# The joint between the two layers of the second MLP: earlier first inputs, later differences and stores, later weight loads, and inputs issued by SyncE

## The chip, the cores and the metric

The kernel runs on one core of a Trainium2 chip. The metric is the device time of one execution in microseconds (us); lower is better. Each kernel is timed in several runs, and one further execution is profiled.

## The reference, cut to what matters

Linear attention over 32 heads, then two MLPs, all in float32:

```python
def phi(x):
    proj = einsum('bhsd,df->bhsf', x, w_phi)
    proj = proj - max(abs(proj), axis=-1)
    return concat([exp(proj), exp(-proj)], axis=-1)
q_p, k_p = phi(q), phi(k)                       # batch 4, 8 heads, 576 tokens, head size 64
num = einsum('bhsf,bhfd->bhsd', q_p, einsum('bhsf,bhsd->bhfd', k_p, v))
x = num / (einsum('bhsf,bhf->bhs', q_p, k_p.sum(2))[..., None] + 1e-6)   # -> 2304 x 512

h = x @ moe_w_in;   x = maximum(0.01 * h, h) @ moe_w_out                 # 512 -> 2048 -> 512
h = x @ moe2_w_in                                                        # 512 -> 2048
sp = where(h > 20, h, log1p(exp(minimum(h, 20))))
out = (h * tanh(sp)) @ moe2_w_out                                        # 2048 -> 512
```

The function between the second MLP's layers, h * tanh(softplus(h)), is called Mish below.

## The kernel before

Every float32 operand of a matmul is cut into a high and a low part, and a product is three matmuls: high by high, high by low, low by high (`three`, lines 95 to 97 of the profile). ScalarE (ACT) rounds the high part (line 91 for inputs, line 262 for weights) and VectorE (DVE) subtracts it to get the low part (line 92 and line 266); this pair is called a split.

The MLPs use a two-by-two block scheme with seven products in place of eight, so sums and differences of blocks stand in for the blocks. The change is about the second MLP. Its first layer runs in 16 items, `cycle(n)`, one for each of eight pairs f of feature blocks and two groups sb of tokens; the last two are item 14 (f = 7, sb = 0) and item 15 (f = 7, sb = 1). The seven products of an item are spread over two calls of `cycle`: the item's last three, `tail4`, `tail5` and `tail3`, run inside the next item. For item 15 they run after the loop, in `first`, with the product `c_item(7)` for the 256 left-over tokens in two halves around `tail3(15)`.

When a block of the first layer is done, ACT applies Mish (line 1424). Three of the four blocks of an item, B11, B21 and B22, are stored to DRAM at once. B12 stays in the tile `g12` (`x1_1`). As soon as the fourth block has come, DVE makes four differences T1, T3, T2, T4 in place (line 1444), and each is stored as well. All these stores are line 1418 (`put`): SyncE (SP) issues the differences, ACT the blocks. In the order listings their targets are called gp, then the group sb, then a number for the block (0 B11, 1 T3, 2 T2, 3 B21, 4 T1, 5 T4, 6 B22), then f // 2. `tail5` also has a DVE addition (line 843) whose result must find a free tile, and such a tile is free when its difference has been stored.

The second layer (`emit_s`) then runs 56 steps, s = 0 to 55, and 8 more for the left-over tokens. A step is 12 matmuls on one input of 128 x 1024 values. The input of step s is read back from DRAM into one of five places (`RAW3`, line 1472, called raw), split in two (called g2), and multiplied with the halves of one block of output weights (called wo2). Step 0 is called input 0 below, and so on. Weights for the last six of the seven phases come as 24 loads of 256 KB (line 1365, called wr), issued by SP into a ring of seven tiles, so that the load of wr n waits for the split of wr n-7.

What sets the order is a counter: each call of `work` is one position, and `later(k, f)` runs f k positions on. The order in which the program emits instructions is the order in which each engine runs them, and each DMA issue stands in its engine's order too. A DMA that has to wait for its source, its target or the DMA issued eight before it (their completion marks are eight, used in turn) holds its engine. The lines that matter: `later(s + 2, lambda s=s: then.load(s))` asks for the first inputs one item before the end, `deep = 3` lets three of them go ahead, and `later(2, lambda: free.add("s0"))` lets the weight loads begin.

Of the kernel before, what the change touches and what calls it, by code (L numbers as in the profile page):

```python
# [20 lines left out]
def attention_two_mlps_kernel(  # L21
# [12 lines left out]
    nc = tc.nc  # L34
# [25 lines left out]
    NF = M // 2  # L60
# [238 lines left out]
    with tc.manual_schedule():  # L299
# [1046 lines left out]
        for f in range(NF):  # L1346
# [3 lines left out]

        PHASES = ((A11, B11, "X"), (S3, T3, "Z"), (S2, T2, "Y"), (A12, B21, "X"), (S1, T1, "Y"), (A22, T4, "W"), (S4, B22, "Y"))
        HOMES = ["s%d" % i for i in range(6, 2 * OPS)] + ["x2_0", "x2_1", "x3_0", "x3_1"] + ["v%d" % i for i in range(9, 14)] \
            + ["xc"] + ["v%d" % i for i in range(4)] + ["x0_0", "x0_1"]
        homes, ready = Lane(5), Lane(1)
        lanes += (homes, ready)
        ready.queue.append(Chain((Stage(0.0, lambda: free.add("v4"), gate="l2",
# [63 lines left out]
        def mish(key, h, g=None):  # L1420
            m, b = key
            if g is None:
                g = role(key)
            nc.scalar.activation(out=g, in_=h, func=AF.Mish)
            if b == B:
                l = gl2[m] = dr.tile([P, 3, NC], F32, name="gl%d" % m)
                later(1, lambda: nc.scalar.dma_start(out=l[:, 0:2].rearrange("p a n -> p (a n)"), in_=g))

                def diff():
                    nc.vector.tensor_tensor(out=g[:, 0:NC], in0=g[:, NC:], in1=g[:, 0:NC], op=ALU.subtract)  # L1430
                    later(1, lambda: nc.sync.dma_start(out=l[:, 2], in_=g[:, 0:NC]))
                later(5, diff)
                return
            f, sb = m // 2, b // 2
            x = mine.setdefault((f, sb), {})
            x[m % 2, b % 2] = g
            if (m % 2, b % 2) != (0, 1):
                o = {(0, 0): B11, (1, 0): B21, (1, 1): B22}[m % 2, b % 2]
                later(1, lambda: put(sb, o, f, g))
                return  # L1440
            b11, b12, b21, b22 = x[0, 0], x[0, 1], x[1, 0], x[1, 1]
            for n, (o, out_, in0, in1) in enumerate(((T1, b11, b12, b11), (T3, b12, b22, b12), (T2, b22, b22, b11), (T4, b21, b21, b22))):
                def sub(o=o, out_=out_, in0=in0, in1=in1):
                    nc.vector.tensor_tensor(out=out_, in0=in0, in1=in1, op=ALU.subtract)
                    later(1, lambda: put(sb, o, f, out_))
                later(n + 1 + (n > 1), sub)

        two_.out, two_.dest = mish, role

        steps3 = [(sb, n, fp) for sb in range(2) for n in range(OPS) for fp in range(NF // 2)] + [(2, 0, f) for f in range(NF)]  # L1450
        NS3 = len(steps3)
        RAW3 = [("cc", gp), ("st0", gp), ("st1", gp), ("x1_0", fix), ("x1_1", fix)]
        PARTS3 = (("s0", "s1"), ("s2", "s3"), ("s4", "s5"))

        class Halves:
# [5 lines left out]
            def load(self, upto):  # L1461
                while self.loaded <= min(upto, NS3 - 1) and self.loaded - self.split_at < self.deep:
# [4 lines left out]
                    t = self.raw[s] = place(tag, F32, 2, MAIN, pool=pool, name="raw2").rearrange("p a n -> p (a n)")  # L1467
                    if sb == 2:
                        t = self.raw[s] = t[:, 0:3 * NC]
                        nc.scalar.dma_start(out=t, in_=gl2[fp].rearrange("p a n -> p (a n)"))  # L1470
                    else:
                        nc.scalar.dma_start(out=t, in_=gs2[sb, PHASES[n][1], fp].rearrange("p a n -> p (a n)"))

            def splits(self, upto):
                while self.split_at <= min(upto, NS3 - 1):
# [115 lines left out]
        def first(n, loads_at, then, few):  # L1591
            for x in items[n + (n > 0):] if n else items:
                if x[0] == "w" or n == 1 and cur[0] is one:
                    cycle(n)
                    n += 1
                    if n == len(it) - 1:
                        for s in range(6):
                            later(s + 2, lambda s=s: then.load(s))
                        if not few:
                            for f in range(NF):  # L1600
                                need("o2", f)
                    loads_at(n)
                if x[0] == "c" and x[1] < NF - 1:
                    c_item(x[1])
# [51 lines left out]

        def gates2(n):
            if n == len(it) - 1:
                later(2, lambda: free.add("s0"))
            if n == len(it):  # L1660
                later(2, lambda: free.add("s1"))

# [67 lines left out]
```

## Time and profile before

| | us |
|---|---|
| median of 3 runs (917.79 to 919.83) | 918.72 |
| the profiled execution | 920.56 |
| its span, first to last instruction | 918.6 |
| TensorE busy in the span | 897.2 (98%) |
| VectorE busy | 625.7 (68%) |
| ScalarE busy | 503.8 (55%) |

The profiled execution is 1.84 us over the median, and 1.96 us of it lie outside the span. Times in rows count from the start of the span. In a timeline a row is: start, length, engine, line, operation, result<-operands, count, and in brackets the idle time ahead of it and what ended that. PE is TensorE, SPq and ACTq are DMA issues of SyncE and ScalarE; the length of a merged row of issues includes the waits between them.

### The profile page before, as it was taken

To read this page: it belongs to the slowest core of one execution; us is meant where nothing else is said; L and a number is where in the kernel's file an instruction comes from. 1 tells how busy PE (TensorE), PEld (TensorE's weight loads), DVE (VectorE), ACT (ScalarE), POOL (GpSimd) and SP (SyncE) were. 2 spreads that over 40 slices of the span, in tenths; PEclk is the share of its full clock that TensorE was granted. 3 is DMA by queue.
4 is the path that set the end of the run, shared out by engine and by line. 5 is a ranking of instruction groups with operands and counts; after the bars stand their busy time and mean duration, and the time that the engine had idled before them with its cause. 6 is when DMAs were issued, how large, how long until landed. Compare 5 with 4: busy or idle time off the path is not lost.

```text
span 918.6 us, 17001 instructions
## 1 busy us (share of the span) xinstructions
PE 897.2 (98%) x6549; PEld 768.5 (84%) x6549; DVE 625.7 (68%) x1056; ACT 503.8 (55%) x827; POOL 68.7 (7%) x36
## 2 busy tenths in 40 slices
PE   8999999999999999999999999999999779999998
PEld 7999999888888888888988888888888658888888
DVE  7899999388888725889882328766654467655552
ACT  5888889566665545454463335544444456454441
POOL 3443443000000000000000000000000000000000
PEclk9999999999999999999999999999999989999999
DMA  7444430258878778799842365889655798886772
GB/s 210 126 102 113 136 106 16 93 182 279 310 262 303 268 226 278 242 356 377 281 137 95 115 218 195 308 300 325 244 218 188 275 364 285 236 238 196 221 195 61
DMA packets 146624, 199.37 MB, mean 217 GB/s; under 512 B 50928, under 2 KB 83312, under 8 KB 146544
## 3 DMA queue, kind: packets, MB, share of 16 engines
q1 hardware_dynamic: 107776, 112.82, 38.6%
q10 hardware_dynamic: 38768, 85.48, 27.2%
q8 instruction: 51, 0.84, 0.4%
q14 instruction: 29, 0.24, 0.1%
HBM read 120.65 MB, written 77.59 MB: 216 GB/s over the span
## 4 chain that ended last, share of the span: by engine, by line
PE 85%; DMA 6%; DVE 4%; ACT 2%; issue 1%; POOL 0%; ACTq 0%; SPq 0%; DVEq 0%
PE a L95 13%; PE a L96 13%; PE a L97 13%; PE b L95 12%; PE b L96 12%; PE b L97 12%; PE outs L491 3%; PE kvp L468 3%; DMA gp<-g 2%; PE a L384 1%; DMA c<-scr 1%; DMA gd<-g 1%; PE xt L516 1%; PE kvp L471 1%; DMA wr<-qd 1%
## 5 line engine op out<-in xcount | busy, mean ns | idle before, releaser
L92 DVE TENSOR_TENSOR g<-raw,g 128x1024 fp32r<-128x1024 f32 (+1 forms) x64 | 76.0, 1189 | 76.5 <-ACT g L91 76.2
L91 ACT ACTIVATE g<-raw 128x1024 fp32r<-128x1024 f32 (+1 forms) x64 | 66.1, 1033 | 81.6 <-PE b L97 39.4
L92 DVE TENSOR_TENSOR gl<-raw,gh 128x512 fp32r<-128x512 f32 x72 | 49.7, 690 | 65.9 <-ACT gh L91 64.7
L91 ACT ACTIVATE gh<-raw 128x512 fp32r<-128x512 f32 x72 | 45.2, 629 | 69.9 <-PE b L97 23.0
L451 POOL PARTITION_ALL_REDUCE qm<-qd x32 | 68.5, 2187 | 88.0 <-ACT qd L446 74.4
L96 PE MATMUL b<-gl,wo 128*128 128x512 f32 (+1 forms) x192 | 68.0, 354 | 0.1
L95 PE MATMUL b<-gh,wo 128*128 128x512 f32 (+1 forms) x192 | 67.9, 354 | 0.0
L97 PE MATMUL b<-gh,wo 128*128 128x512 f32 (+1 forms) x192 | 67.9, 354 | 0.0
L95 PE MATMUL b<-win,w 128*128 128x512 f32 x128 | 50.2, 392 | 3.6 <-DVE g L843 3.6
L96 PE MATMUL b<-win,w 128*128 128x512 f32 x128 | 49.9, 390 | 0.0
L97 PE MATMUL b<-win,w 128*128 128x512 f32 x128 | 49.8, 389 | 0.0
L95 PE MATMUL a<-gh,wo 128*128 128x512 f32 x128 | 49.8, 389 | 0.0
L96 PE MATMUL a<-gl,wo 128*128 128x512 f32 x128 | 49.8, 389 | 0.0
L97 PE MATMUL a<-gh,wo 128*128 128x512 f32 x128 | 49.8, 389 | 0.0
L95 PE MATMUL b<-g,wo 128*128 128x512 f32 x128 | 49.8, 389 | 0.0
L96 PE MATMUL b<-g,wo 128*128 128x512 f32 x128 | 49.8, 389 | 0.0
L97 PE MATMUL b<-g,wo 128*128 128x512 f32 x128 | 49.8, 389 | 0.0
L843 DVE TENSOR_TENSOR g<-b,z 128x512 f32<-128x512 f32 x31 | 21.4, 689 | 40.9 <-PE b L97 38.1
L96 PE MATMUL a<-g,wo 128*128 128x512 f32 x96 | 39.1, 407 | 7.3 <-DVE g L92 7.3
L96 PEld LDWEIGHTS b<-gl,wo 128*128 128x128 f32 x192 | 36.3, 189 | 5.4 <-DVE gl L92 0.5
L95 PEld LDWEIGHTS b<-gh,wo 128*128 128x128 f32 x192 | 36.3, 189 | 5.2
L97 PEld LDWEIGHTS b<-gh,wo 128*128 128x128 f32 x192 | 36.3, 189 | 5.0
(302 smaller groups left out, 2569.5 us busy)
## 6 DMA issues: line engine op xcount, KB each, us to landing
raw<-gp ACTq DMA_DIRECT2D x56, 512.0 KB, 4.4
raw<-gd ACTq DMA_DIRECT2D x72, 256.0 KB, 3.3
gd<-g ACTq DMA_DIRECT2D x71, 256.0 KB, 3.7
stage<-in_moe_w_in_dram SPq DMA_DIRECT2D x32, 512.0 KB, 5.6
stage<-in_moe_w_out_dram SPq DMA_DIRECT2D x32, 512.0 KB, 5.2
gp<-g SPq DMA_DIRECT2D x64, 256.0 KB, 2.8
gp<-g ACTq DMA_DIRECT2D x48, 256.0 KB, 2.8
more<-scr SPq DMA_DIRECT2D x24, 256.0 KB, 4.4
```

The lines of the kernel that those rows point to most:

```text
L91: nc.scalar.activation(out=hi, in_=src, func=AF.Copy)
L92: nc.vector.tensor_tensor(out=lo, in0=src, in1=hi.bitcast(F32), op=ALU.subtract)
L95: nc.tensor.matmul(out=o, lhsT=wh_, rhs=xh, start=start, stop=False, **kw)
L96: nc.tensor.matmul(out=o, lhsT=wh_, rhs=xl, start=False, stop=False, **kw)
L97: nc.tensor.matmul(out=o, lhsT=wl_, rhs=xh, start=False, stop=stop, **kw)
L384: nc.tensor.transpose(out=t[:, j * P:(j + 1) * P], in_=s[nm + "n"].rearrange("p h t d -> p (h t d)")[:, j * P:(j + 1) * P], identity=ident)
L451: nc.gpsimd.partition_all_reduce(qm, qd, P, bass_isa.ReduceOp.absmax)
L468: nc.tensor.matmul(out=both[r, h, a, :], lhsT=s["kp"][a][:, h, t, r], rhs=s["vm"][:, h, t, :], start=(a == 0 and h == 0 and t == 0), stop= ...
L471: nc.tensor.matmul(out=both[r, :, a, :], lhsT=l["lp"][a][:, i % 2, r], rhs=s["vl"], start=False, stop=(a == 1), skip_group_check=True)
L491: nc.tensor.matmul(out=g[r, u // 2, u % 2, h], lhsT=s["qp"][a][:, h, q0 + r.start:q0 + r.stop], rhs=s["kv"][:, 2 * h + a], start=(a == 0), ...
L516: nc.tensor.transpose(out=t[:, j * P:(j + 1) * P], identity=ident, in_=s["xn"].rearrange("p c m d -> p c (m d)")[:, j // 2, (j % 2) * P:(j ...
L843: nc.vector.tensor_tensor(out=c, in0=x["Y"], in1=cur[0].z7[n % 2], op=ALU.add)
```

## The change

Six edits, all at the joint of the two layers of the second MLP:

- The first three inputs are asked for one item sooner, after `cycle(13)` in place of `cycle(14)`, at positions 1, 3 and 5. Since their places hold the last weights of the first layer until these are split, `need` asks first that this has been done.
- Inputs are issued by SP in place of ACT, all 64 of them.
- The fifth place for inputs is `x0_0`, which held weights of the first layer, in place of `x1_1`, which is the tile `g12`; the last two weight homes change accordingly.
- The four differences of item 15 are made 10, 14, 18 and 22 positions later, in place of 1, 2, 4 and 5.
- The stores of item 15's B21 and B22 are issued 10 and 12 positions later, in place of 1.
- The weight loads are let go 5 positions later, in place of 2.

```diff
-            + ["xc"] + ["v%d" % i for i in range(4)] + ["x0_0", "x0_1"]
+            + ["xc"] + ["v%d" % i for i in range(4)] + ["x0_1", "x1_1"]
...
-                later(1, lambda: put(sb, o, f, g))
+                later(1 if (f, sb) != (NF - 1, 1) or o == B11 else 10 if o == B21 else 12, lambda: put(sb, o, f, g))
...
-                later(n + 1 + (n > 1), sub)
+                later(n + 1 + (n > 1) if (f, sb) != (NF - 1, 1) else 10 + 4 * n, sub)
...
-        RAW3 = [("cc", gp), ("st0", gp), ("st1", gp), ("x1_0", fix), ("x1_1", fix)]
+        RAW3 = [("cc", gp), ("st0", gp), ("st1", gp), ("x1_0", fix), ("x0_0", fix)]
...
-                        nc.scalar.dma_start(out=t, in_=gl2[fp].rearrange("p a n -> p (a n)"))
+                        nc.sync.dma_start(out=t, in_=gl2[fp].rearrange("p a n -> p (a n)"))
                     else:
-                        nc.scalar.dma_start(out=t, in_=gs2[sb, PHASES[n][1], fp].rearrange("p a n -> p (a n)"))
+                        nc.sync.dma_start(out=t, in_=gs2[sb, PHASES[n][1], fp].rearrange("p a n -> p (a n)"))
...
-                    if n == len(it) - 1:
+                    if few and n == len(it) - 1:
                         for s in range(6):
                             later(s + 2, lambda s=s: then.load(s))
-                        if not few:
-                            for f in range(NF):
-                                need("o2", f)
+                    if not few and n == len(it) - 2:
+                        for f in range(NF):
+                            need("o2", f)
+                        for i in range(4):
+                            need("w2", NF - 1, i)
+                        for s in range(3):
+                            later(2 * s + 1, lambda s=s: then.load(s))
...
             if n == len(it) - 1:
-                later(2, lambda: free.add("s0"))
+                later(5, lambda: free.add("s0"))
```

TensorE's order of instructions is the same before and after. SP's order around item 14 is, before (gl is a store for the left-over tokens):

```order
L1418 DMA gp0_1_3_8245<-g12_6919 128x512
L1418 DMA gp0_2_3_8271<-g_8182 128x512
L1418 DMA gp0_5_3_8281<-g_8141 128x512
L1431 DMA gl6_8248<-left_6964 128x256
L1418 DMA gp1_4_3_8330<-g_8205 128x512
L1418 DMA gp1_1_3_8344<-g12_6919 128x512
L1365 DMA wr_8346<-qd3_0_7049 128x512
L1365 DMA wr_8348<-qd3_1_7283 128x512
L1365 DMA wr_8350<-qd3_2_7525 128x512
L1365 DMA wr_8352<-qd3_3_7764 128x512
L1365 DMA wr_8354<-qd5_0_7051 128x512
L1418 DMA gp1_2_3_8378<-g_8289 128x512
```

and after:

```order
L1472 DMA raw2_8233<-gp0_0_0_6837 128x1024
L1418 DMA gp0_1_3_8247<-g12_6919 128x512
L1472 DMA raw2_8260<-gp0_0_1_7262 128x1024
L1418 DMA gp0_2_3_8275<-g_8182 128x512
L1472 DMA raw2_8285<-gp0_0_2_7714 128x1024
L1418 DMA gp0_5_3_8287<-g_8141 128x512
L1431 DMA gl6_8250<-left_6964 128x256
L1418 DMA gp1_4_3_8336<-g_8205 128x512
L1418 DMA gp1_1_3_8348<-g12_6919 128x512
L1418 DMA gp1_2_3_8368<-g_8295 128x512
L1418 DMA gp1_5_3_8379<-g_8257 128x512
L1365 DMA wr_8382<-qd3_0_7049 128x512
```

The three first inputs stand among the stores of item 12, and the last two stores of item 13 (gp1_2_3, gp1_5_3) stand ahead of the five weight loads.

DVE's order from the split of input 1 to that of input 2 is, before (g_8373 and g_8327 are tiles of item 14; g_8398, g_8426 and g_8415 of item 15):

```order
L92 TENSOR_TENSOR g2_8465<-raw2_8365,g2_8464 128x1024
L1444 TENSOR_TENSOR g_8373<-g_8373,g_8309 128x512
L1444 TENSOR_TENSOR g_8398<-g12_6919,g_8398 128x512
L266 TENSOR_TENSOR wo2_8434<-wr_8346,wo2_8434 128x512
L266 TENSOR_TENSOR wo2_8436<-wr_8348,wo2_8436 128x512
L266 TENSOR_TENSOR wo2_8438<-wr_8350,wo2_8438 128x512
L1444 TENSOR_TENSOR g_8327<-g_8327,g_8373 128x512
L1444 TENSOR_TENSOR g12_6919<-g_8426,g12_6919 128x512
L266 TENSOR_TENSOR wo2_8440<-wr_8352,wo2_8440 128x512
L266 TENSOR_TENSOR wo2_8442<-wr_8354,wo2_8442 128x512
L1444 TENSOR_TENSOR g_8426<-g_8426,g_8398 128x512
L1444 TENSOR_TENSOR g_8415<-g_8415,g_8426 128x512
```

and after, with the split of input 2 as its last row:

```order
L92 TENSOR_TENSOR g2_8454<-raw2_8260,g2_8453 128x1024
L1444 TENSOR_TENSOR g_8365<-g_8365,g_8315 128x512
L1444 TENSOR_TENSOR g_8333<-g_8333,g_8365 128x512
L266 TENSOR_TENSOR wo2_8476<-wr_8382,wo2_8476 128x512
L266 TENSOR_TENSOR wo2_8478<-wr_8384,wo2_8478 128x512
L266 TENSOR_TENSOR wo2_8480<-wr_8386,wo2_8480 128x512
L92 TENSOR_TENSOR g2_8504<-raw2_8285,g2_8503 128x1024
```

Eleven instructions stand between the two splits before, five after.

The load of input 3 stands on ACT before, between the split of input 2 and that of input 3:

```order
L91 ACTIVATE g2_8518<-raw2_8376 128x1024
L1472 DMA raw2_8529<-gp0_0_3_8120 128x1024
L1472 DMA raw2_8531<-gp0_1_0_6960 128x1024
L1472 DMA raw2_8533<-gp0_1_1_7407 128x1024
L1472 DMA raw2_8535<-gp0_1_2_7859 128x1024
L91 ACTIVATE g2_8544<-raw2_8529 128x1024
```

After, it is the last row of this piece of SP's order (the tiles of the first two stores are g_8365 and g_8333 of the DVE rows above):

```order
L1418 DMA gp0_2_3_8275<-g_8365 128x512
L1418 DMA gp0_5_3_8287<-g_8333 128x512
L1365 DMA wr_8488<-qd5_1_7285 128x512
L1365 DMA wr_8490<-qd5_2_7527 128x512
L1365 DMA wr_8493<-qd5_3_7766 128x512
L1365 DMA wr_8509<-qd1_0_6939 128x512
L1365 DMA wr_8511<-qd1_1_7177 128x512
L1472 DMA raw2_8519<-gp0_0_3_8120 128x1024
```

It has left ACT, and stands on SP behind the stores of item 14's T2 and T4 and five weight loads.

## Rows read from the trace of the kernel before

**Rows 1.** The page, 40 equal slices of the span.
```profile
PE   8999999999999999999999999999999779999998
PEclk9999999999999999999999999999999989999999
```

**Rows 2.** Busy time by stretch: length, engines, granted clock, DMA share, GB/s.
```profile
720.00:730.00 10.00, 6.38 (x33) 4.80 (x31) 1.92 (x2) 6.21 (x11) 0.00 (x0) 1.00 0.69 245
730.00:740.00 10.00, 4.33 (x15) 3.08 (x16) 9.41 (x14) 1.53 (x2) 0.00 (x0) 0.91 0.78 261
740.00:750.00 10.00, 8.38 (x25) 5.56 (x25) 4.08 (x5) 5.80 (x9) 0.00 (x0) 0.75 1.00 362
...
800.00:840.00 40.00, 40.00 (x178) 33.11 (x177) 20.58 (x19) 19.43 (x24) 0.00 (x0) 1.00 0.80 232
```

**Rows 3.** TensorE's timeline through the joint.
```profile
717.33 0.39 PE L95 MATMUL b<-win,w 128*128 128x512 f32 x1
...
718.69 0.28 PE L95 MATMUL a<-c,w 128*128 128x256 f32 x1
...
720.00 0.28 PE L97 MATMUL a<-c,w 128*128 128x256 f32 x1
722.83 0.50 PE L95 MATMUL b<-win,w 128*128 128x512 f32 x1 [2.55 <-DVE g L843]
...
739.19 0.80 PE L96 MATMUL a<-g,wo 128*128 128x512 f32 x1 [4.87 <-DVE g L92]
739.78 0.63 PE L97 MATMUL a<-g,wo 128*128 128x512 f32 x1
...
744.05 0.63 PE L95 MATMUL a<-g,wo 128*128 128x512 f32 x1
...
752.26 0.39 PE L95 MATMUL a<-g,wo 128*128 128x512 f32 x1
```

**Rows 4.** The chain of waits, 715 to 760: start, length, what.
```profile
712.08 9.91 DMA gp<-g
...
733.13 2.87 DMA wr<-qd
...
737.13 3.96 DMA gp<-g
741.19 5.99 DMA raw<-gp
```

**Rows 5.** DVE's timeline.
```profile
722.08 0.69 DVE L843 TENSOR_TENSOR g<-b,z 128x512 f32<-128x512 f32 x1 [2.61 <-DMA gp<-g]
...
732.37 1.89 DVE L266 TENSOR_TENSOR wo<-wr,wo 128x512 fp32r<-128x512 f32 x3
...
737.91 1.22 DVE L92 TENSOR_TENSOR g<-raw,g 128x1024 fp32r<-128x1024 f32 x1
```

**Rows 6.** DMA issues of SP.
```profile
709.13 2.85 SPq L1365 DMA_DIRECT2D wr<-qd  x5
```

**Rows 7.** ACT's timeline.
```profile
717.42 0.60 ACT L1424 ACTIVATE g<-b 128x512 f32<-128x512 f32 x1 [0.62 <-DMA wr<-qd]
...
726.39 2.18 ACT L262 ACTIVATE wo<-wr 128x512 fp32r<-128x512 f32 x4
...
730.90 11.58 ACTq L1472 DMA_DIRECT2D raw<-gp  x4
742.58 1.06 ACT L91 ACTIVATE g<-raw 128x1024 fp32r<-128x1024 f32 x1 [10.65 <-DMA gp<-g]
```

**Rows 8.** The inputs' tile, raw, 700 to 765: from issue to landing.
```profile
DMA to landing us min/median/max: 3.6/6.0/8.6
```

**Rows 9.** The same tile, 765 to 893.
```profile
DMA to landing us min/median/max: 2.9/4.3/6.4
```

**Rows 10.** DMA of 738 to 741: SP's queue (q1), the only one that moved anything.
```profile
DMA packets 627, 1.15 MB, mean 382 GB/s; under 512 B 67, under 2 KB 67, under 8 KB 627
...
q1 hardware_dynamic: 627, 1.15, 100.9%
```

## The prediction

> **What bounds the kernel now.** The page comes first. TensorE is busy nine tenths or more in nearly every slice, except the first, the last, and two in the last quarter at seven tenths, the second of them with a lower granted clock [rows 1]. So only a change of that place can move much. The busy time by stretch narrows it to 720 to 750: from 730 to 740 TensorE works 4.33 of 10 us while VectorE works 9.41, and from 740 to 750 the granted clock is 0.75 [rows 2]. This is the joint that the diff touches.
>
> TensorE's timeline gives what is lost there. Six matmuls of 512 columns take 1.36 us, 0.227 each (717.33 to 718.69), and those of 256 columns follow each other at 0.119 (eleven from 718.69 to 720.00) [rows 3]. From 718.69 to the start of step 5 at 752.26 stand 24 of the small ones and 66 of the large (six of item 15's last product and 12 for each of steps 0 to 4): 24 x 0.119 + 66 x 0.227 = 17.8 us of work in 33.6 us. **So 15.7 us are lost**, and step 5 could at best start at 736.5.
>
> The chain of waits and the timelines of DVE and ACT say to whom. (1) The 2.55 us ahead of 722.83 are item 15's last product waiting for the addition of `tail5` [rows 3], which waited for a store [rows 5]; this store took 9.91 us to land, from 712.08 [rows 4]. It stood behind five weight loads, issued from 709.13 on [rows 6]. (2) The 4.87 us ahead of 739.19 are the low part of input 2 [rows 3]: DVE made it only at 737.91, after the differences of items 14 and 15 and five weight splits [rows 5]. (3) In it the clock fell: 739.78 to 744.05 is ten matmuls at 0.427 us, so some twelve cost 0.2 us each more, 2.4 us [rows 3]. (4) ACT stood in the issue of input 4 until 742.58 [rows 7], since its place was `g12`, whose store left only at 737.13 and took 3.96 us; the load itself took another 5.99 [rows 4], and step 4 came late by it. Small waits for splits make up the rest.
>
> **The change, part by part.** I work the new joint through from 718.69, TensorE's order being the same, with durations from rows: Mish 0.60 (717.42), a weight's high part 0.55 (four in 2.18), an input's high part 1.06 [rows 7]; a difference or an addition about 0.69, a weight's low part 0.63 (three in 1.89), an input's low part 1.22 [rows 5]; a weight load takes SP 0.57 to issue (five in 2.85) [rows 6].
>
> *First inputs earlier, by SP; weight loads later.* Inputs 0 to 2 now go out among item 12's stores, more than 10 us before the weight loads of 709.13, and the last two stores of item 13 stand ahead of these loads. Three loads and five weight loads, 2.8 MB, no longer meet with those stores. SP is held by nothing new there except for a fraction of a us of issues; the stores that it shifts free tiles that are next written an item later, and I cost this at nothing; without that cover it would be 0.57 per issue. The addition of `tail5` then runs when its product ends at 718.9, and TensorE's 2.55 us go: first half of the left-over product to 720.12, last product of item 15 to 721.48, second half to 722.91, step 0 to 725.63, step 1 to 728.35.
>
> *Differences of item 15 put off.* Next is the order on ACT and DVE. Item 15's last block ends at 721.65, Mish to 722.25, input 1's high part to 723.3, low part to 724.55; step 1 has it in time. DVE goes on with T2 and T4 of item 14 (725.2, 725.85) and three weights (727.75). ACT does the left-over Mish, a store's issue (0.4) and five high parts of weights, to 727.1, then input 2's high part to 728.2; its low part is there at 729.45, not at 737.9. Step 2 loses 0.8 us (its second matmul starts 729.45, not 728.6) and ends at 731.95. The put-off differences (four, 2.8 us) and stores are read only by the second group of tokens, 28 steps later; on DVE they fall into steps 3 to 11.
>
> *Input 3 and the fifth place.* What is late next is input 3. It now stands on SP behind the store of T2(14), which cannot go before 725.2. Queued behind it are the store of T4(14), five weight loads and inputs 3 to 6, and TensorE waits for input 3. So: stores at 725.2 and 725.85, five weight loads from 726.25 at 0.57 each, input 3 issued at 729.1. No row of before shows this queue; the landing of an input in the busy stretch took 3.6 us at least, 6.0 at the median and 8.6 at most [rows 8]. I take 6.0: the nearest row is input 4, also behind stores and weight loads, with 5.99 [rows 4]. So it lands at 735.1; high part 736.15, low part 737.4; step 3's second matmul starts there, eleven more bring 739.95, and step 4 ends at 742.65. With the places of inputs 3 and 4 freed by 721.7, input 4 follows 1.3 us behind input 3 (524 KB at 382 GB/s [rows 10]) and its low part is ready before 739.9.
>
> The Trainium skill, "DMA: Bandwidth & Descriptors", section "Queues, rings and completion order", says that SP and ACT each own one ring on the same 16 DMA engines, that an engine takes turns between rings and works one ring in order; that speaks against taking the inputs off ACT's ring. No run here shows the two side by side. By it input 3 waits for the 1.84 MB ahead of it, and 2.36 MB at 382 GB/s begun 2.2 us after 725.2 (a weight load with little beside it landed in 2.87, 0.67 of them for its own 256 KB [rows 4]) have landed at 733.6; the sum would be 1.5 us lower than by the median.
>
> *Later steps.* From step 5 on the margin is thin: working on by the same durations, with the put-off differences in between, the low part of input 6 ends near 745.2 against a need at 745.6, that of input 7 at 748.4 against 748.35. I cost it at nothing; the cover is DVE's free time, some 0.6 us in each step of 2.72 with its low parts.
>
> *64 issues off ACT.* ACT is not late after 752, so this saves nothing there. On SP they stand among stores of the output. An input needs to be there five steps of 2.72 us after its issue by the program's order, 13.6 us, against 2.9 to 6.4 for landing [rows 9]; nothing.
>
> **The sum.** Step 5 starts at 742.65 in place of 752.26: 9.6 us less, of 15.7 lost. On the profiled execution that is 920.56 - 9.6 = 911.0; it was 1.84 us above the median, so for runs **918.72 - 9.6 = 909.1 us**. With input 3 landing after 3.6 us it is 906.7, after 8.6 us 911.7.
>
> **The rivals.** *The clock falls again.* TensorE idles some 4.2 us ahead of step 3 and a further 1.1 behind its first matmul. In the trace 2.55 us of idling left the granted clock at 1.00, that is 2.4 GHz, and 4.87 came with a fall to half of it [rows 2, 3]. Ours lies between. Then the 2.4 us are paid once more: 911.5. The Trainium skill, "TensorE: Matmul & The Clock Gate", Part 1, says that the throttled clock is the default and activity releases it, which the row of 739.78 agrees with.
>
> *A new wait behind step 5.* If DVE or the one queue falls behind by a step, each of steps 6 to 9 may wait 0.5 to 1 us: 911 to 913. For it: DVE was 9.41 busy of 10 with a like mix [rows 2]. Against: this mix held eleven instructions between two splits, the new one at most five.
>
> *Slower.* All inputs, weights and output stores now share one queue. The DMA was busy 0.80 of the time in 800 to 840 with both [rows 2]. If one queue alone had less than 0.8 of the rate of both, inputs would bound the whole layer: at 0.7 the stretch of 40 us would take 32 / 0.7 = 45.7, so the 128 us from 760 to 888 some 18 more, and the time is 909.1 + 18 = 927; below 0.74 the change is a loss. Against: SP's queue alone moved 382 GB/s at full share [rows 10].
>
> *Nothing gained.* If input 3 were held on SP as long as ACT was (until 741), steps 3 on would stand where they stood: 918 to 919. The place that held ACT is gone from the list, so this is unlikely.
>
> **How the numbers follow.** Forecast with input 3 landing anywhere between its bounds, 0.56; clock 0.20; new wait 0.12; slower 0.05; nothing gained 0.03; better than the lower bound, with input 3 in time, 0.04. The range goes from the forecast's lower bound, 906.7, to 912.5, past the clock case and into the new waits; what is left out is about 0.2. Runs of this kernel can tell 0.2%, 1.8 us: all cases but two are faster by more, so faster 0.92, same 0.03, slower 0.05.
>
> **What would show it.** In the trace after: TensorE without a wait from 700 to 728; `tail5`'s addition on DVE near 718.9; the low part of input 2 near 728.2; one large gap of 3 to 5 us ahead of step 3, ended by the load of input 3, issued near 729; no wait after step 5; granted clock 1.00 there, or a second dip. A gap ahead of step 0, an issue of input 3 after 732, or waits repeating every few steps would make the sum wrong.

## The result and the profile after the change

The changed kernel takes 911.0 us, the median of four runs (910.47 to 912.50), against 919.28 us for the kernel before in its four (917.79 to 920.17). The ratio is 0.9914, with a 95% interval of 0.9895 to 0.9933: 0.9% faster, 8.3 us of medians. Forecast were 909.1 us and a range of 906.7 to 912.5, so the sign, the size and the range held; the forecast itself was 1.9 us too low.

The page of the profiled execution (910.47 us, span 908.4), the two rows that answer to [rows 1]:

```profile
PE   8999999999999999999999999999999979999998
PEclk9999999999999999999999999999999999999999
```

Of the two slices at seven tenths one is left, and none has a visibly lower clock. The busy time by stretch (length; PE, PEld, DVE, ACT and POOL busy with their counts; granted clock; DMA share; GB/s) answers to [rows 2]:

```profile
720.00:730.00 10.00, 9.68 (x47) 7.63 (x46) 7.09 (x10) 5.61 (x9) 0.00 (x0) 1.00 0.66 213
730.00:740.00 10.00, 5.01 (x15) 3.67 (x15) 5.45 (x7) 6.34 (x10) 0.00 (x0) 0.83 1.01 382
740.00:750.00 10.00, 10.00 (x46) 8.29 (x45) 7.46 (x10) 6.55 (x9) 0.00 (x0) 1.00 0.99 362
800.00:840.00 40.00, 40.00 (x178) 33.14 (x177) 20.55 (x19) 18.89 (x21) 0.00 (x0) 1.00 0.77 232
```

TensorE now works 9.68 of the first ten us and all of the third; what is lost lies in 730 to 740, where the granted clock is 0.83 as well. Its timeline there answers to [rows 3]; the first row is the first matmul of the left-over product, 718.69 before:

```profile
716.88 0.28 PE L95 MATMUL a<-c,w 128*128 128x256 f32 x1
...
727.32 0.50 PE L96 MATMUL a<-g,wo 128*128 128x512 f32 x1 [0.33 <-DVE g L92]
...
734.39 0.51 PE L95 MATMUL a<-g,wo 128*128 128x512 f32 x1 [4.24 <-ACT g L91]
735.65 0.80 PE L96 MATMUL a<-g,wo 128*128 128x512 f32 x1 [0.75 <-DVE g L92]
...
738.79 0.40 PE L97 MATMUL a<-g,wo 128*128 128x512 f32 x1
...
742.42 0.39 PE L95 MATMUL a<-g,wo 128*128 128x512 f32 x1
```

The bracketed ones are all the waits of TensorE from 700 to the end; the last row is the first matmul of step 5. The gap of 2.55 us for `tail5` is gone; of the 4.87 for input 2 there are 0.33 left; one gap of 4.24 us has come ahead of step 3, and 0.75 behind its first matmul. From 735.65 to 738.79 stand seven spacings, 3.14 us, most of them 0.43, where the full clock gives 0.227.

What the other engines show there, DVE first, then ACT, then SP's issues (answers to [rows 5, 6, 7]):

```profile
717.09 0.69 DVE L843 TENSOR_TENSOR g<-b,z 128x512 f32<-128x512 f32 x1 [0.67 <-PE b L97]
726.04 1.22 DVE L92 TENSOR_TENSOR g<-raw,g 128x1024 fp32r<-128x1024 f32 x1 [0.20 <-ACT g L91]
```
```profile
733.28 1.06 ACT L91 ACTIVATE g<-raw 128x1024 fp32r<-128x1024 f32 x1 [7.27 <-DMA raw<-gp]
```
```profile
715.72 8.67 SPq L1418 DMA_DIRECT2D gp<-g  x4
724.48 2.71 SPq L1365 DMA_DIRECT2D wr<-qd  x5
727.28 2.33 SPq L1472 DMA_DIRECT2D raw<-gp  x4
```

The addition of `tail5` waits for its product and no longer for a store. Input 2's low part follows its high part at once. Input 3, the first of the four loads of 727.28, stands on SP behind the stores of item 14's T2 and T4 (the end of the row of 715.72, which includes the wait for DVE) and five weight loads, and ACT starts its high part at 733.28, 6.0 us after the issue.

**How the kernels are compared below.** The profiled executions differ in the first 20 us, where nothing was changed. Matmuls of 256 columns in the first products of the program, of the kernel before and then of the changed one:

```profile
7.14 0.41 PE L95 MATMUL a<-wbh,kth 128*128 128x256 f32 x1
```
```profile
6.81 0.28 PE L95 MATMUL a<-wbh,kth 128*128 128x256 f32 x1
```

By the spacing of the matmuls (0.21 against 0.12 us there; the rows give a granted clock of 1.00 for both) the half speed of the start lasted to 11 us in one and to 5 in the other, which is worth 1.6 us in code that is the same. So beside the medians each kernel's **tail** is given: from the first matmul of the left-over product to the end of the span. It is 918.6 - 718.69 = 199.9 us before and 908.4 - 716.88 = 191.5 after, 8.4 less; the remaining 1.8 of the two spans' 10.2 lies ahead of the joint. A tail is that of one execution, which need not be a typical one: the profiled one of "inputs by ACT" took 911.07 us, 2.4 over its median. In the last column a positive number is a longer tail than the changed kernel's.

| kernel | median of runs | ratio to before [interval] | span | left-over product begins | tail | against changed |
|---|---|---|---|---|---|---|
| before | 919.28 | | 918.6 | 718.69 | 199.9 | +8.4 |
| changed | 911.0 | 0.9914 [0.9895, 0.9933] | 908.4 | 716.88 | 191.5 | |
| inputs 3 and 4 early | 906.18 | 0.9861 [0.9848, 0.9873] | 904.3 | 718.13 | 186.2 | -5.3 |
| inputs by ACT | 908.65 | 0.9897 [0.9883, 0.9912] | 909.0 | 717.91 | 191.1 | -0.4 |
| gap filled with 15 matmuls | 911.67 | 0.9916 [0.9902, 0.9930] | 910.2 | 718.59 | 191.6 | +0.1 |
| both gaps filled | 908.68 | 0.9892 [0.9879, 0.9906] | 906.7 | 716.81 | 189.9 | -1.6 |
| weight loads as before | 911.57 | 0.9916 [0.9903, 0.9929] | 909.9 | 718.23 | 191.7 | +0.2 |
| first inputs as before | 912.1 | 0.9919 [0.9906, 0.9933] | 910.6 | 718.79 | 191.8 | +0.3 |
| both as before | 917.55 | 0.9985 [0.9974, 0.9996] | 916.9 | 718.89 | 198.0 | +6.5 |
| differences as before | 914.8 | 0.9955 [0.9943, 0.9968] | 912.4 | 718.55 | 193.9 | +2.3 |
| differences and place as before | 914.31 | 0.9948 [0.9936, 0.9961] | 912.3 | 718.52 | 193.8 | +2.3 |
| SP alone, on the kernel before | 920.64 | 1.0018 [1.0009, 1.0028] | 918.4 | 717.60 | 200.8 | +9.3 |
| inputs 3 to 6 early | 906.44 | 0.9862 [0.9848, 0.9875] | 904.1 | 717.49 | 186.6 | -4.9 |

### The profile page after: what moved, and what is told of

Same layout as the page of the kernel before. It is cut to its first block, busy times and chain, and to the rows that moved or that the text cites. A ratio compares the mean times of both kernels' runs of the same rounds, so it can differ in the third digit from the quotient of the medians.

```text
span 908.4 us, 17014 instructions
## 1 busy us (share of the span) xinstructions
PE 892.3 (98%) x6549; PEld 766.1 (84%) x6549; DVE 625.6 (69%) x1056; ACT 503.6 (55%) x827; POOL 68.7 (8%) x36
## 4 chain that ended last, share of the span: by engine, by line
PE 91%; DVE 4%; DMA 1%; ACT 1%; issue 1%; POOL 0%; ACTq 0%; SPq 0%; DVEq 0%
PE a L95 14%; PE b L95 14%; PE a L96 14%; PE b L96 13%; PE a L97 13%; PE b L97 13%; PE outs L491 3%; PE kvp L468 3%; PE a L384 1%; PE xt L516 1%; PE kvp L471 1%; DMA raw<-gp 1%; POOL qm L451 0%; PE kvp L520 0%; DVE mx L408 0%
```

## The experiments

### What is left: input 3's place on SP

After `tail3(15)` inputs 3 and 4 are asked for at once, with the limit of three loads ahead lifted:

```diff
+        def ahead(then):
+            then.deep = len(RAW3)
+            then.load(4)
...
-            c_item(NF - 1, lambda: (tail3(n - 1), then.splits(-2 if few else 1), work()), work, ...
+            c_item(NF - 1, lambda: (tail3(n - 1), few or ahead(then), then.splits(-2 if few else 1), work()), work, ...
```

> From the changed kernel (911.0 us). Inputs 3 and 4 are issued right behind the last product of item 15, ahead of the stores of T2(14) and T4(14) and of the five weight loads, so some 7 us sooner. Theory (what is left in the joint is input 3's place on SP's queue): the gaps of 4.24 and 0.75 us ahead of and in step 3 go, the granted clock stays at 1.00 and the 1.3 us that half the clock cost go too: 911.0 - 6.3 = 904.7, ratio to the kernel before 0.984. Rival 1 (the DMA engines are full there, so input 3 only takes the landing time of what is shifted behind it, and the weight loads or input 5 are waited for instead): a gain of at most 2 us, 909 to 911, ratio 0.989 to 0.991, with a new gap ahead of one of steps 3 to 6. Rival 2 (the gap goes but the clock falls all the same): 906.0, ratio 0.9855, and a granted clock under 1.00 between 730 and 745.

Measured: 906.18 us, ratio 0.9861; the tail is 5.3 us shorter than in the changed kernel. SP issues the two inputs at 721.14, 3.0 us behind the left-over product's first matmul, where it was 10.4. This is SP's row; then come TensorE's waits, all but the 0.33 of step 2, and two stretches:

```profile
721.14 1.48 SPq L1472 DMA_DIRECT2D raw<-gp  x2
```
```profile
737.39 0.50 PE L96 MATMUL a<-g,wo 128*128 128x512 f32 x1 [0.36 <-DVE g L92]
740.89 0.50 PE L96 MATMUL a<-g,wo 128*128 128x512 f32 x1 [0.45 <-DVE g L92]
```
```profile
730.00:740.00 10.00, 9.63 (x42) 7.62 (x42) 6.34 (x9) 6.25 (x10) 0.00 (x0) 1.00 1.02 387
740.00:750.00 10.00, 9.55 (x41) 7.32 (x41) 9.81 (x13) 7.69 (x12) 0.00 (x0) 1.00 1.03 389
```

Both gaps at step 3 are gone, and the granted clock is 1.00. So the theory holds: the 5.3 us that were left hung on where inputs 3 and 4 stand in SP's order. Of the 6.3 us expected some 1 us was given back, in the two new waits, for the low parts of inputs 5 and 6: they are the first rival's, at a smaller price, in a stretch in which the DMA engines are full (387 GB/s at a share of 1.02). This version is faster than both kernels.

### Inputs 5 and 6 early as well

The edit is against the version above; `ahead` now takes the last input to ask for as an argument:

```diff
-            c_item(NF - 1, lambda: (tail3(n - 1), few or ahead(then), then.splits(-2 if few else 1), work()), work, ...
+            c_item(NF - 1, lambda: (tail3(n - 1), few or ahead(then, 4), then.splits(-2 if few else 1), few or ahead(then, 6), work()), work, ...
```

> The changed kernel with inputs 3 and 4 issued behind the last product of item 15, as in the run that gave 906.2 us, and inputs 5 and 6 too, behind the split of input 1, so ahead of the stores of T2(14) and T4(14) and of five weight loads. The run with 3 and 4 had three waits left in the joint, 0.33, 0.36 and 0.45 us ahead of steps 2, 5 and 6. Theory (the last two are input 5, issued at 729.25 and landed at 735.0, too late for its step): they go, 906.2 - 0.8 = 905.4, ratio 0.985, and TensorE waits for nothing from step 3 on. Rival (SP now stands until input 1's place is free, and the five weight loads behind it are late for steps 9 to 13, or the landing of inputs 3 and 4 slows down): a new wait of 0.5 to 2 us, 906.2 to 908.

Measured: 906.44 us, the same as with inputs 3 and 4 alone; the tail is 0.4 us longer. The rival is right, with a mechanism that was not in it. DVE's and TensorE's rows:

```profile
730.17 0.43 DVE L1430 TENSOR_TENSOR left<-left 128x256 f32<-128x256 f32 x1 [1.10 <-DMA gl<-left]
```
```profile
731.78 0.50 PE L96 MATMUL a<-g,wo 128*128 128x512 f32 x1 [0.84 <-DVE g L92]
```

The wait at step 5 is gone (the one at step 6 is not), but the difference of the left-over tokens now waits on DVE for a small store, issued by ACT, that lands beside four inputs in place of two, 7.6 us after its issue; the low part of input 3 is queued behind it, and step 3 waits 0.84 us. In this stretch, where the DMA engines are full, moving two loads ahead made another transfer late.

### The clock: filling the gap

Added to the changed kernel, ahead of step 3, on data that are at hand (input 2's high part), into the bank of the left-over product, which is free by then:

```diff
...
             sb, n, fp = steps3[s]
+            if s == 3:
+                g = s3.parts[2][0]
+                for _ in range(15):
+                    nc.tensor.matmul(out=spare_bank[0], lhsT=g[:, 0:P], rhs=g[:, 0:MAIN], start=True, stop=True)
             emit_s(s, 0)
```

> The changed kernel (911.0 us) with work added: 15 matmuls of 512 columns, 3.4 us at the full clock, on input 2's high part stand ahead of step 3, where TensorE idles 4.24 us; nothing uses their product. Theory (the clock fell because TensorE idled): the granted clock stays at 1.00 between 730 and 745 and the eight matmuls that ran at half clock take 1.8 in place of 3.14 us, so the time falls by 1.3 us although work is added: 909.7, ratio 0.9895. Rival (the clock falls there for another reason, or the remaining gap is enough): the dip stays, the time stays at 911.0 or rises by up to 0.5, ratio 0.991 to 0.992.

Measured: 911.67 us, tail +0.1: no gain. TensorE's timeline:

```profile
731.69 3.56 PE L1680 MATMUL a<-g 128*128 128x512 f32 x15
736.01 0.50 PE L95 MATMUL a<-g,wo 128*128 128x512 f32 x1 [0.76 <-ACT g L91]
737.27 0.50 PE L96 MATMUL a<-g,wo 128*128 128x512 f32 x1 [0.76 <-DVE g L92]
...
738.31 0.63 PE L97 MATMUL a<-g,wo 128*128 128x512 f32 x1
...
741.30 0.59 PE L95 MATMUL a<-g,wo 128*128 128x512 f32 x1
```

In this execution the clock fell all the same, a little later. But the six runs differ: three had a mean granted clock of 0.997 and took 912.2 to 912.7 us, this one among them, and three had 0.999 or 1.000 and took 908.8 to 911.2. So the fall differs between executions of one kernel, and the median hides it. Also, two gaps of 0.76 us were left, so this doesn't decide between theory and rival. In a further kernel both gaps are closed: 19 matmuls ahead of step 3 and 4 between its first and second.

> The changed kernel (911.0 us) with work added, more than in the run with 15 matmuls: 19 matmuls of 512 columns ahead of step 3 and 4 behind its first matmul, 5.2 us at the full clock, so that both gaps of 4.24 and 0.75 us are closed but for some 0.2 us each; nothing uses their product. The run with 15 had two gaps of 0.76 us left and the clock still fell for 3.4 us. Theory (idling is what the clock falls for, and 1.5 us of it were enough there): the granted clock stays at 1.00 from 720 to 760 and the time from the joint's begin to the end is 1.3 us shorter than in the changed kernel, less what the added matmuls delay step 3, 0.2: some 910, ratio 0.990. Rival (the fall has another cause than TensorE's idling): half clock for 3.4 us again, 911 to 912.

Measured: 908.68 us, tail 1.6 us shorter, with 5.2 us of work added. TensorE's timeline and the stretch:

```profile
729.87 4.47 PE L1498 MATMUL a<-g 128*128 128x512 f32 x19
...
734.41 1.09 PE L1498 MATMUL a<-g 128*128 128x512 f32 x4
735.34 0.49 PE L1516 MATMUL a<-g,wo 128*128 128x512 f32 x1
```
```profile
730.00:740.00 10.00, 10.00 (x45) 7.98 (x44) 5.74 (x7) 6.83 (x11) 0.00 (x0) 1.00 0.99 373
```

With next to no idling the granted clock stayed at 1.00, that is 2.4 GHz, although input 3's high part came only 0.25 us sooner (16.15 us behind the left-over product's start, 16.40 in the changed kernel). The mean granted clock was 0.999 to 1.000 in all four runs, 0.996 to 0.998 in the four of the changed kernel. So in the changed kernel the fall followed from TensorE's idling. Of the 1.6 us some 1.4 are the clock, near the 1.3 expected: the seven spacings that took 3.14 us at half clock take 1.72 here; the rest is input 3's 0.25. The Trainium skill, "TensorE: Matmul & The Clock Gate", Part 1, says that activity releases the throttle; the run with both gaps closed agrees.

### One edit undone: who issues the inputs

```diff
-                        nc.sync.dma_start(out=t, in_=gs2[sb, PHASES[n][1], fp].rearrange("p a n -> p (a n)"))
+                        nc.scalar.dma_start(out=t, in_=gs2[sb, PHASES[n][1], fp].rearrange("p a n -> p (a n)"))
```

(and the same for the left-over tokens' loads)

> From the changed kernel (911.0 us) with one edit undone: the 64 inputs are issued by ACT again; places, positions, differences and weight loads stay as changed. Theory (what held ACT before was the place g12 of input 4, not the issuing itself): ACT is not held, input 3 is issued by ACT behind input 2's high part, at 726.1 in place of 727.3 of the changed kernel's span, and step 3 starts up to 1.2 us sooner: 909.8 to 911.0, ratio 0.990 to 0.991. Rival (issuing by SP is itself what freed ACT): ACT stands for several us in a row of issues of inputs 3 to 6 as it did before, the high part of input 3 is late and step 3 or 4 loses 2 to 5 us: 913 to 916, ratio 0.993 to 0.996. For the later steps both expect no change, since ACT has free time there; a loss of 1 us or more spread over 760 to 890 would speak for one queue being better than two.

Measured: 908.65 us, below the theory's 909.8 to 911.0; in the profiled execution, at 911.07 one of the two longest of five, the tail is 0.4 us shorter than in the changed kernel. The way there was not the theory's. Two pieces of this kernel's chain of waits (start, length, what), ACT's rows and TensorE's:

```profile
726.35 5.66 DMA wr<-qd
732.09 0.33 ACTq L1472
```
```profile
723.53 0.33 ACTq L1472 DMA_DIRECT2D raw<-gp  x1
...
732.52 1.06 ACT L91 ACTIVATE g<-raw 128x1024 fp32r<-128x1024 f32 x1 [5.48 <-DMA wr<-qd]
```
```profile
733.62 0.50 PE L95 MATMUL a<-g,wo 128*128 128x512 f32 x1 [2.48 <-ACT g L91]
734.88 0.79 PE L96 MATMUL a<-g,wo 128*128 128x512 f32 x1 [0.76 <-DVE g L92]
...
740.17 0.63 PE L96 MATMUL a<-g,wo 128*128 128x512 f32 x1
```

ACT issued input 3 5.6 us behind the left-over product's start, where SP does it 10.4 behind, and then stood in the issue of the inputs behind it until a weight load had landed, so that input 3's high part began only at 732.52. The inputs use nothing of that load, so it was most likely its completion mark that was waited for; the trace doesn't tell. That is the rival's mechanism: issuing on ACT does hold ACT, 5.5 us here, with no part of the place in it. Its price, against the changed kernel, is nothing, since there input 3 is later still: the gap ahead of step 3 is 2.48 us in place of 4.24. Of these 1.8 us some 1.3 went to the clock: 13 matmuls at half clock in place of 7, 0.2 us each. That is this execution; the two runs with a granted clock of 1.000 took 908.0 and 908.2 us, the two with 0.995 and 0.996 911.1 and 911.3. So issuing by SP is not shown to gain anything here, and the medians lean the other way. Later steps, 2.72 us each, show no loss in either version. Two queues against one, DMA totals of 726 to 735 here and of 727 to 735 in the changed kernel:

```profile
DMA packets 1515, 3.29 MB, mean 366 GB/s; under 512 B 170, under 2 KB 298, under 8 KB 1513
...
q1 hardware_dynamic: 1152, 1.97, 57.7%
q10 hardware_dynamic: 361, 1.31, 41.8%
```
```profile
DMA packets 1088, 2.87 MB, mean 359 GB/s; under 512 B 120, under 2 KB 120, under 8 KB 1088
...
q1 hardware_dynamic: 1088, 2.87, 98.6%
```

Side by side the two queues (q1 SP's, q10 ACT's) share the engines, and together move about what one moves alone, 366 against 359 GB/s. The Trainium skill, "DMA: Bandwidth & Descriptors", section "Queues, rings and completion order", says that SP's and ACT's rings are on the same 16 DMA engines; the trace agrees.

### One edit undone, or two: first inputs and weight loads

First inputs one item later again, still by SP; then, in another kernel, weight loads let go 2 positions on (`later(2, ...)`); then both together. The core of the first:

```diff
-                    if few and n == len(it) - 1:
+                    if n == len(it) - 1:
                         for s in range(6):
                             later(s + 2, lambda s=s: then.load(s))
-                    if not few and n == len(it) - 2:
...
-                        for s in range(3):
-                            later(2 * s + 1, lambda s=s: then.load(s))
```

> From the changed kernel (911.0 us) with one edit undone: the first three inputs are asked for one item later, as before, still issued by SP. Theory A (the 2.55 us wait for tail5's addition came from the inputs and weight loads meeting with item 13's stores; the later weight loads alone clear the way): no wait ahead of the last product of item 15, input 0 lands in time for step 0, and the time is 911 to 911.5, ratio 0.991 to 0.9915. Theory B (1.5 MB of inputs between these stores are enough to hold them up): 1 to 2.6 us of that wait come back, 912 to 913.6, ratio 0.992 to 0.994.

Measured: 912.1 us, tail +0.3. Theory A: the addition of `tail5` runs 0.67 us of waiting behind its product, at 718.99, as in the changed kernel.

> From the changed kernel (911.0 us) with one edit undone: weight loads are let go 2 positions on, as before, in place of 5. Theory A (the early first inputs alone had cleared the way for the stores of item 13): the addition of tail5 is not late, and the time is 911.0 or up to 1 us lower, since three of the five weight loads that stood ahead of input 3 are issued sooner, ahead of the store of T2(14): ratio 0.990 to 0.991. Theory B (the five weight loads ahead of the last two stores of item 13 made that addition late): the gap of 2.55 us behind the first half of the left-over product comes back, 913 to 913.6, ratio 0.9935, less what a sooner input 3 gives back.

Measured: 911.57 us, tail +0.2. Theory A again on `tail5`, but what an earlier start of the weight loads was to bring did not come. SP's and TensorE's rows:

```profile
718.21 8.74 SPq L1365 DMA_DIRECT2D wr<-qd  x3
```
```profile
730.76 0.50 PE L96 MATMUL a<-g,wo 128*128 128x512 f32 x1 [2.34 <-DVE g L92]
```

Their ring has seven tiles, so SP stood in these three issues until wr 0 was split; the store of T2(14) and input 3 were behind. And ACT split five weights ahead of input 1, so that input 2's low part was 2.34 us late; the gap ahead of step 3 shrank to 0.51 + 0.77. The loss had moved from one step to another. So the later weight loads are part of what brings input 2 in time.

> From the changed kernel (911.0 us) with two edits undone together: the first inputs are asked for one item later and the weight loads are let go 2 positions on, both as before; each alone cost at most 0.3 us of the joint and brought no wait for tail5's addition back. Theory (either edit alone takes away the meeting of inputs, weight loads and item 13's last two stores; the second then finds nothing left): together the wait of 2.55 us ahead of item 15's last product is back, and 1.5 to 2.9 us of it remain at the end: 912.5 to 914, ratio 0.993 to 0.9945. Rival (the wait came with the inputs on ACT or with the early differences): no such wait, 911 to 912.

Measured: 917.55 us, tail +6.5, far beyond the theory's 2.9 at most. DVE, SP and TensorE:

```profile
723.94 0.69 DVE L843 TENSOR_TENSOR g<-b,z 128x512 f32<-128x512 f32 x1 [5.52 <-DMA gp<-g]
```
```profile
719.63 13.86 SPq L1365 DMA_DIRECT2D wr<-qd  x3
```
```profile
724.69 0.79 PE L95 MATMUL b<-win,w 128*128 128x512 f32 x1 [4.20 <-DVE g L843]
```

The wait for `tail5` is back, at 4.20 us and not 2.55, and the clock falls behind it and again later (22 matmuls at half clock in place of 7). So the mechanism was right, its price not. With the other edits in place the two are substitutes: each alone clears the way for item 13's last stores, so undoing one shows next to nothing, and undoing both gives back 6.5 of the 8.4 us. Either alone on the kernel before was not tried.

### Two more edits undone: differences and place

The four differences and the stores of B21 and B22 go back together, so the two are not told apart:

```diff
-                later(1 if (f, sb) != (NF - 1, 1) or o == B11 else 10 if o == B21 else 12, lambda: put(sb, o, f, g))
+                later(1, lambda: put(sb, o, f, g))
...
-                later(n + 1 + (n > 1) if (f, sb) != (NF - 1, 1) else 10 + 4 * n, sub)
+                later(n + 1 + (n > 1), sub)
```

> From the changed kernel (911.0 us) with one edit undone: the four differences of item 15 and the stores of its B21 and B22 stand at their old positions again; the fifth place x0_0 stays. Theory (putting them off freed DVE for input 2's low part and SP for input 3): the four differences, 2.8 us, stand on DVE ahead of input 2's low part, which is there near 730 in place of 727.3 of the changed kernel's span, and their stores stand on SP ahead of the five weight loads and of input 3, which is issued 2 to 3 us later. Of the two the later decides: +2 to +4 us, 913 to 915, ratio 0.9935 to 0.9955, with a wait of TensorE ahead of the second matmul of step 2. Rival (DVE had room enough and input 3 hangs on T2 and T4 of item 14 alone): 911 to 912, ratio 0.991 to 0.9925.

Measured: 914.8 us, tail +2.3, inside the theory's bounds. TensorE and SP:

```profile
731.10 0.50 PE L96 MATMUL a<-g,wo 128*128 128x512 f32 x1 [2.45 <-DVE g L92]
```
```profile
731.13 1.88 SPq L1472 DMA_DIRECT2D raw<-gp  x4
```

The low part of input 2 is late by the differences, and input 3 is issued 731.13 - 718.55 = 12.6 us behind the left-over product's start, 10.4 in the changed kernel: 2.2 later, and this is what the tail shows.

Then the fifth place for inputs is the tile of `g12` again, and the weight homes stand as before:

```diff
-        RAW3 = [("cc", gp), ("st0", gp), ("st1", gp), ("x1_0", fix), ("x0_0", fix)]
+        RAW3 = [("cc", gp), ("st0", gp), ("st1", gp), ("x1_0", fix), ("x1_1", fix)]
```

> As the run with the differences of item 15 at their old positions, and in addition the fifth place for inputs is the tile of g12 again (x1_1) and the weight homes stand as before; the place can't be undone without the differences. What stays of the change: the first inputs sooner, SP for all inputs, the weight loads later. Theory (the place held the queue that issues input 4, and all behind it): SP now stands in the issue of input 4 until the store of g12's difference T1(15) has landed, as ACT did until 742.58 before, and input 4's high part comes after 740: another +2 to +4 us over the run with the differences alone, 915 to 918, ratio 0.996 to 0.999, with a wait ahead of step 4. Rival (with the stores of item 13 and the weight loads out of the way, g12's store lands soon and the place holds nobody): the same time as the run with the differences alone, within 0.7 us.

Measured: 914.31 us, the same tail as with the differences alone. The rival is right: the four inputs are issued in one go, 1.89 us as above, and none waits for the place.

### One edit alone on the kernel before

The kernel before with `nc.sync` in place of `nc.scalar` for the inputs.

> The kernel before (919 us) with one edit of the change alone: the inputs are issued by SP. Theory (SP brings nothing by itself): the 2.55 us wait stays, the differences stay ahead of input 2's low part, and input 3 now stands on SP behind the stores of item 15's four differences, the last of which DVE makes only near 735; ACT is free instead, so its splits of weights come sooner. 917 to 921, ratio 0.998 to 1.002. Rival (ACT's standing in the issue of input 4 until 742.58 was what cost steps 3 and 4, and SP alone takes it away): 3 to 5 us less, 914 to 916, ratio 0.9945 to 0.997.

Measured: 920.64 us, ratio 1.0018 (1.0009 to 1.0028). TensorE's waits for `tail5` and for input 2, and SP's issue of input 3:

```profile
722.48 0.79 PE L95 MATMUL b<-win,w 128*128 128x512 f32 x1 [3.29 <-DVE g L843]
...
737.90 0.50 PE L96 MATMUL a<-g,wo 128*128 128x512 f32 x1 [3.99 <-DVE g L92]
```
```profile
737.15 4.91 SPq L1472 DMA_DIRECT2D raw<-gp  x4
```

SP brings nothing by itself: by the interval it costs 0.8 to 2.6 us. The same edit undone in the changed kernel points the same way (908.65 against 911.0), though the intervals overlap there. With SP, differences and place together (the kernel with both other edits undone) it is 917.55, and with either of those two edits 911 to 912.

## Why the prediction held, and the step that did not

Times of the changed kernel's span get 1.8 us added here, the difference of the two spans ahead of the joint, to stand beside those of the prediction.

- **What bounds the kernel.** The joint was the place, and nothing behind it moved: no wait of TensorE from step 4 to the end, as before from step 5 on, but for 0.3 us in step 5.
- **`tail5`'s 2.55 us.** Gone as forecast: the addition at 717.09 + 1.8 = 718.9, as forecast. The reason given, loads and stores that no longer meet, holds; that one of the two edits would have done was not seen.
- **Input 2.** Its low part ends at 727.26 + 1.8 = 729.06, forecast 729.45. With the differences at their old places the wait is 2.45 us, and with the weight loads let go early it is 2.34. So it took both edits; the prediction named only the differences for it.
- **Input 3.** Issued at 729.08 (forecast 729.1), 6.0 us to its high part (forecast 6.0 to land), second matmul of step 3 at 735.65 + 1.8 = 737.45 (forecast 737.4). So the choice of the median landing, from the nearest row [rows 8, 4], was right, and the landing of 733.6 that the sentence beside it worked out was 1.5 us too early. The place of inputs 3 and 4 on SP held nearly all that was left: with the two early the tail is 5.3 us shorter.
- **The step that failed: the clock.** The sum took "TensorE idles some 4.2 us ahead of step 3 and a further 1.1 behind its first matmul" as not enough for a fall, and kept the fall as a rival at 0.20 and 2.4 us. It idled 4.24 and 0.75, and the clock fell: in the profiled execution for 7 matmuls, not some 12, and the seven spacings above took 3.14 us in place of 7 x 0.227 = 1.59. These 1.55 us (1.42 of them the clock, as the same seven take 1.72 with both gaps closed) are the difference between step 5's forecast start, 742.65, and 742.42 + 1.8 = 744.22 in the trace: 8.0 us of gain there in place of 9.6, to which 0.3 more came in step 5, where the kernel before had a last small wait. The profiled execution was the mildest of the four: its mean granted clock is 0.998, that of the other three 0.996, which is also that of the kernel before's profile. So there the fall was longer, probably as long as the rival had it; no trace shows it. The rival's 911.5 came nearer to the 911.0 than the forecast did. That 911.0 lies within the forecast's own bounds, 906.7 to 911.7, is luck: they were drawn for the landing of input 3, which came out as forecast, and not for the clock. The rows before allowed either: 2.55 without a fall, 4.87 with one [rows 2, 3].
- **The place.** Loss (4) of the prediction put ACT's standing until 742.58 down to the place `g12`. For the kernel before the rows bear that out: the store of the difference in it left only at 737.13, and input 4 went when it had landed [rows 4]. But the new place is not what the change gained by. With the new place and inputs on ACT, ACT is held 5.5 us all the same, behind a weight load; and with the old place and the differences early nobody waits for it. There the new place is worth nothing; whether it is needed once the differences are put off was not tried.
- **The rivals.** A new wait behind step 5 did not come: the thin margins at inputs 6 and 7 held. The shared queue cost nothing: DMA share 0.77 in 800 to 840 against 0.80 [rows 2], and landing from 765 us on at the median 4.5 us, against 4.3 [rows 9], where 13.6 are at hand:

```profile
DMA to landing us min/median/max: 3.8/4.5/7.3
```

## To carry to other kernels

Where a load that an engine waits for is issued in program order, look at what it is queued behind, not only at when its place is free: here one load stood behind two stores, which waited for DVE, and five loads that nobody needed yet, and asking for it and the next one sooner took 5.3 us off a kernel that the whole change had made 8.4 us faster. Undo edits in pairs, too: two edits that remove the same collision each look worthless when undone alone. And a gap on TensorE is priced with the clock that may fall behind it, and its price neither follows the gap's length alone nor is the same in every execution.

## What the runs showed of the hardware

- The fall of the clock doesn't go by the length of one idle stretch: 2.55 us [rows 3] and 0.36 and 0.45 us (inputs 3 and 4 early) were followed by none; 2.34 us (weight loads as before) by one from 731.34 on; 2.45 us ahead of the same matmul of step 2 by none until the next gap (differences as before) and by one at 732.57 (differences and place as before); two of 0.76 us, one matmul apart (15 matmuls added), by one of 3.4 us, about as long as the 3.1 behind 4.24 and 0.75. Behind 2.48 and 0.76 (inputs by ACT) it lasted nearly twice as long, 5.7 us. So shortening a gap may give back to the clock most of what it saves in waiting, 1.3 of 1.8 us there; what decides it these runs leave open.
- Nor is it the same in every execution of one kernel: the five runs with inputs by ACT had a mean granted clock of 0.995, 0.996, 0.998, 1.000 and 1.000, and those at 1.000 were some 3 us shorter than those at 0.995 and 0.996 (part of it may be the start).
- Work whose result nobody uses (23 matmuls, 5.2 us) made the tail 1.6 us shorter, 1.4 of them because TensorE kept its clock.
- At the start of the program matmuls ran at half speed, by their spacing, until 5 to 12 us, in executions of code that is the same there. Between the profiles before and after that is worth 1.6 us: as much as an edit of the joint.
